# A written-out instruction order replanned: VectorE's SBUF steps given a later planned start beside GpSimd, and one weight load held back

## The chip, the cores and the metric

The kernel runs on one core of a Trainium2 chip. The time is device microseconds from start to end of one execution; for each kernel the median of several runs is given. Lower is better. The engines are named as in the profile: PE is TensorE (matmul), DVE is VectorE, ACT is ScalarE, POOL is GpSimd, SP is SyncE, which issues most DMAs here.

## The reference

The reference is one transformer-like block on 4096 positions of 640 channels, in float32. A first network mixes positions in the frequency domain; a second one is a gated feed-forward network. Both sit behind a layer norm that is scaled and shifted by a condition vector `c`, and both are added back through a gate. Cut to what matters:

```python
mod = (silu(c) @ w_mod).reshape(1, 6, 1, 640)        # sa, ca, ga, sb, cb, gb
h = layernorm(x) * (1 + ca) + sa
z = rfft2(h)                                          # 4096 positions, 4 blocks of 160 channels
h1 = relu(z @ w1 + b1); o = softshrink(h1 @ w2 + b2)  # complex, block by block
x = x + ga * irfft2(o)
h = layernorm(x) * (1 + cb) + sb
x = x + gb * ((silu(h @ w_gate) * (h @ w_up)) @ w_down)   # 640 -> 1728 -> 640
```

## The kernel before, in words

TensorE multiplies in a reduced float32 format. To keep full accuracy, every operand is split in two: ScalarE writes the rounded high part (`high`), VectorE subtracts it from the original and writes the low part (`low`), and each product is made of three matmuls (high x high, high x low, low x high). A product therefore needs one VectorE operation with two inputs in SBUF for each of its operands. The many L1481 (`wb`, gate and up weights), L1671 and L1680 (down weights), L1748 (`chl`, frequency rows), L1870 (`ho`, left sides), L2125, L2274 and L2157 (activations) lines of the profile are such differences.

The first network fills the first 300 us or so of the profile. The change does not touch it. The second network goes through five tiles of rows (`TL`: two of 512 rows, three of 1024). In each tile it goes through 14 units of gate and up weights (`WG`; unit 4 is the up weight of the second pair of column blocks) and seven pieces of down weights. The seventh piece is the narrow rest: rows 1536 to 1727 of `w_down`. From the third tile on a variant with seven products in place of eight is used for most blocks; it needs sums and differences of blocks, which GpSimd makes.

At the same time the rows of the next tile are prepared. For each row, the frequency-domain result is read back (`cr`), multiplied by the gate on GpSimd (L1741, `gated`), split, transformed on TensorE (L1758), added to `x` on VectorE (L1762), normed, transposed, split again (L1870), written to DRAM (`hs`) and read back as the left side `h` of the next tile (L1951).

All of this stands in one instruction order which the Python program writes out by hand with a planner. It keeps a clock `now` (TensorE's planned time), the planned time at which each engine is free (`free["A"]`, `["V"]`, `["P"]` for GpSimd, `["S"]` for SyncE), and the planned end of each step (`done`). Side work is put into `Chain`s of `Step(engine, duration, function, deps, key, ...)`. After each stretch of matmuls `slot` moves the clock and `sweep` goes through the chains in a fixed order: `tries` emits a chain's first step if what it depends on is planned to be done by about now and if its engine could start it no later than `AHEAD` (0.9 us for VectorE and SyncE, 1.2 us for GpSimd) from now. A step that TensorE needs at once is emitted by `until` and `force`. TensorE's own side work (engine `"T"`: L1758 and the transposes) is emitted only some time after its inputs are planned to be ready. Operations that read TensorE's results are emitted directly and planned by `core`. Nothing of the planner runs on the chip: it only decides in which order each engine's queue is filled. On the chip each engine works through its queue in that order and waits at semaphores for its data.

`prep_wd(t, p)` makes the steps for piece `p` of the down weights in tile `t`. For the narrow rest in the first tile (`own`) these are: a load in three DMAs (L1655, L1657), two folds on GpSimd that multiply the gate vector into the weights (L1662), four conversions on ScalarE (L1682), four differences on VectorE (L1680) and a store of the folded weights for later tiles (L1685). The chain `first_w` that holds them is the last in the order of the chains. Before the change its load depends on nothing, so it is planned first of all. The key `("wb", 0, 4, 1)` is the second half of the split of unit 4 in the first tile.

Of the kernel before, what the change touches and what calls it, by code (L numbers as in the profile page):

```python
# [13 lines left out]
P = 128  # L14
D = 640
S = 4096
# [158 lines left out]
def body(tc, x, w1, b1, w2, b2, wg, wu, wd, c, wm, k_fa, k_tb, k_tx, k_bx, k_ga, k_ge, k_id, out, dbg=None):  # L175
    nc = tc.nc
    pe, act, dve, pool = nc.tensor, nc.scalar, nc.vector, nc.gpsimd
# [27 lines left out]
    with ExitStack() as top:  # L205
# [34 lines left out]
        with ExitStack() as af:  # L240
# [351 lines left out]
            wdf = {}  # L592
# [552 lines left out]
        with ExitStack() as ff:  # L1145
# [37 lines left out]
            now = [0.0]  # L1183
            free = dict.fromkeys("AVPSDG", 0.0)
# [11 lines left out]
            bufs |= {f"p{q}": 2 for q in range(4)}  # L1196
            room = {k: [0.0] * n for k, n in bufs.items()}

            class Step:
                def __init__(self, e, n, f, deps=(), key=None, use=(), free=(), bulk=0.0):  # L1200
                    self.e, self.n, self.f, self.deps, self.key = e, n, f, deps, key
                    self.use, self.free, self.bulk = use, free, bulk

            class Chain:
# [25 lines left out]
                def run(self):  # L1230
                    t = self.at()
                    st = self.steps.pop(0)
                    for tag in st.use:
                        room[tag].remove(min(room[tag]))
                    e = st.e
                    if e == "T":
                        wait_pe(t)
                        st.f()
                        now[0] += st.n
                        end = now[0] + 0.17 + LAT  # L1240
                    elif e == "N":
                        end = t
                    elif e in "SG":
                        q = "S" if e == "S" else "P"
                        issue = max(free[q], now[0], t) + (0.45 if e == "S" else 0.6)
                        st.f()
                        free[q] = issue
                        free["D"] = max(free["D"], issue + 0.9) + st.n
                        end = free["D"] + 0.9
                    else:  # L1250
                        start = max(free[e], now[0], t)
                        st.f()
                        free[e] = start + st.n
                        end = free[e] + LAT
                    if st.key is not None:
                        done[st.key] = end
                    for tag in st.free:
                        room[tag].append(end)

            def wait_pe(t):  # L1260
                if t > now[0]:
                    now[0] = t + min(2.0, t - now[0])

            def tries(c):
                while c.steps:
                    st = c.steps[0]
                    e = st.e
                    t = c.at()
                    if t is None or t > now[0] + (EARLY[e] if e != "T" else -0.8 if ("tile", NS) in done else
                                                  -1.8 if st.deps[0][0] == "xn" else -0.8):  # L1270
                        return
                    if e == "T" and not (room["p1"] or room["p2"] or room["p3"]):
                        return
                    if e not in "TN":
                        start = max(free["P" if e == "G" else e], now[0], t)
                        if start > now[0] + AHEAD[e]:
                            return
                        if e == "A" and start + st.n > quiet[0] + 0.45:
                            return
                        if st.bulk and free["D"] > now[0] + st.bulk:  # L1280
                            return
                    c.run()
# [9 lines left out]
            def sweep():  # L1292
                held = False
                for c in tails + chains:
                    if c in rows:

                        if held:
                            continue
                        tries(c)
                        held = len(c.steps) > 0  # L1300
                    else:
                        tries(c)
                tails[:] = [c for c in tails if c.steps]
# [249 lines left out]
            wds = {}  # L1553
# [77 lines left out]
            def prep_wd(t, p):  # L1631
                if (t, min(p, NPR - 1)) in D7:
                    return block_loads(t, p)
                made = t or p < 4

                own = t == 0 and p == NPR
# [48 lines left out]
                    nc.sync.dma_start(wdd[p], wdraw[t, p].rearrange("p a b -> p (a b)"))  # L1685

                raw_ = ("wdr", t, p)
                out = [Step("S", 1.7, load, (("wds", p),) if made else (), raw_, ("h4", "h7", "e") if own else ("wd",))]
                for f in range(0 if made else 2):
                    out += [Step("P", 2.2, lambda f=f: fold(f), (raw_, ("gbb", 0), ("gbb", 1)), ("wdg", p, f))]  # L1690
                ready = (raw_,) if made else (("wdg", p, 0), ("wdg", p, 1))
# [5 lines left out]
                for f in range(0 if p == NPR else 2):  # L1697
# [3 lines left out]
                                 free=("wd",) if f and made else ())]  # L1701
# [916 lines left out]
            for t in range(NT):  # L2618
                for p in range(NPR + 1):
                    (first_w if (t, p) == (0, NPR) else down_w).add(prep_wd(t, p))  # L2620
                if t >= NS:
                    for n in range(NW):
                        if WG[n][0] != "s":
                            wtl.add([load_t(t, n, i) for i in range(2)])
                if t:
                    left_l.add(load_h(t))
                    x2_l.add(load_x2(t))
                    row_chain(t)
# [55 lines left out]
```

## Time and profile before

| what | value |
|---|---|
| median of 3 runs before | 1421.38 us (1418.54 to 1427.64) |
| the profiled execution, its own time | 1417.8 us |
| its span, first to last instruction | 1415.7 us |
| TensorE busy | 1380.6 us |
| VectorE busy | 1075.7 us |
| ScalarE busy | 698.0 us |
| GpSimd busy | 517.5 us |
| HBM read and written | 233.37 MB and 104.86 MB |

A line of a timeline gives the start and the length in us, the engine, the line of the kernel, the operation, output <- inputs, shape and count, and in brackets how long the engine had stood idle and for whom. Lines of several like instructions are merged (`x2`); their length then runs from the first start to the last end. A line of the view of waits gives the total, the number and the longest of the waits. A line of the table of windows gives the busy time of each engine in the window, the granted TensorE clock, the busy share of the DMA engines and GB/s. In the list of DMA issues the last column is the median time from issue to landing.

### The profile page before, as it was taken

What the parts mean: (1) busy time and instruction counts of PE and PEld (TensorE: products, weight loads), DVE (VectorE), ACT (ScalarE), POOL (GpSimd) and SP (SyncE); (2) the same over time, 40 slices, a digit from 0 to 9 for tenths busy, and PEclk for the clock granted to TensorE, in tenths of its full rate; (3) what the DMA queues carried; (4) which work ended last, traced back from release to release, by engine and by line L of the source; (5) the groups of instructions that cost most, each with busy time, mean ns of one, the idle gap of its engine ahead of it and who ended that gap; (6) DMA issues with size and microseconds to landing.
All of it is one profiled execution on the core that took longest, in us unless ns stands there. A gap on an engine that the chain in (4) does not pass through costs nothing.

```text
span 1415.7 us, 22483 instructions
## 1 busy us (share of the span) xinstructions
PE 1380.6 (98%) x8096; PEld 1205.4 (85%) x8096; DVE 1075.7 (76%) x1882; ACT 698.0 (49%) x1350; POOL 517.5 (37%) x592
## 2 busy tenths in 40 slices
PE   6999999989999999998999999999999999999998
PEld 2699999968888888887889888888888898888888
DVE  8888898798888799758787786476677756666666
ACT  6855555555454565544554455354443415443431
POOL 5300330135474355222444344232434403555431
PEclk9999999999999999999999999999999999999999
DMA  9976677557769978996766779974664795444441
GB/s 373 321 246 207 213 245 241 190 166 263 258 225 333 340 260 301 364 363 217 238 206 238 236 243 359 351 245 159 211 200 142 251 362 202 149 144 153 162 143 75
DMA packets 135519, 339.71 MB, mean 240 GB/s; under 512 B 19152, under 2 KB 56080, under 8 KB 129648
## 3 DMA queue, kind: packets, MB, share of 16 engines
q1 hardware_dynamic: 127264, 322.15, 65.7%
q0 software_dynamic: 6272, 12.85, 2.8%
q10 hardware_dynamic: 1872, 3.28, 0.6%
q8 instruction: 64, 1.05, 0.3%
q14 instruction: 47, 0.39, 0.1%
HBM read 233.37 MB, written 104.86 MB: 239 GB/s over the span
## 4 chain that ended last, share of the span: by engine, by line
PE 82%; DVE 10%; DMA 4%; issue 2%; ACT 1%; POOL 0%; SPq 0%; DVEq 0%; ACTq 0%; POOLq 0%
PE pd L2543 13%; PE pw L2224 8%; PE pw L2226 8%; PE pw L2225 8%; PE pc L803 5%; PE pd_X L2406 5%; PE pl L735 5%; PE pg L2090 3%; PE pg L2089 3%; PE pg L2088 3%; PE pd_Y L2406 2%; PE pw L2237 2%; PE pw L2235 2%; PE pw L2236 2%; PE pb L639 2%
## 5 line engine op out<-in xcount | busy, mean ns | idle before, releaser
L2543 PE MATMUL pd<-wdh,a 128*128 128x320 f32 x896 | 205.7, 310 | 0.5 <-DVE x L2512 0.5
L1481 DVE TENSOR_TENSOR wb<-r,wb 128x512 fp32r<-128x512 f32 (+3 forms) x133 | 147.1, 1111 | 11.9 <-ACT wb L1478 11.7
L2543 PEld LDWEIGHTS pd<-wdh,a 128*128 128x128 f32 x896 | 151.8, 188 | 1.6 <-DVE x L2512 0.8
L2543 PE MATMUL pd<-wdl,a 128*128 128x320 f32 x448 | 138.4, 309 | 0.0
L2512 DVE TENSOR_TENSOR x<-x,pd 128x320 f32<-128x320 f32 x224 | 101.9, 478 | 34.9 <-PE pd L2543 30.2
L2224 PE MATMUL pw<-h,wt 128*128 128x512 f32 x312 | 124.3, 399 | 3.4 <-ACT s_x L2243 2.2
L2226 PE MATMUL pw<-h,wt 128*128 128x512 f32 x312 | 122.4, 392 | 0.0
L2225 PE MATMUL pw<-h,wt 128*128 128x512 f32 x312 | 122.1, 391 | 0.0
L1478 ACT ACTIVATE wb<-r 128x512 fp32r<-128x512 f32 (+3 forms) x141 | 97.2, 705 | 33.0 <-PE pw L2237 22.8
L2090 PE MATMUL pg<-ht,wb 128*128 128x512 f32 x260 | 101.5, 390 | 3.2 <-DVE wb L1481 3.2
L2088 PE MATMUL pg<-ht,wb 128*128 128x512 f32 x260 | 102.7, 395 | 0.0
L2089 PE MATMUL pg<-ht,wb 128*128 128x512 f32 x260 | 101.5, 390 | 0.0
L2226 PE MATMUL pw<-h,wb 128*128 128x512 f32 x234 | 91.3, 390 | 1.5 <-DVE wb L1481 1.5
L2224 PE MATMUL pw<-h,wb 128*128 128x512 f32 x234 | 91.4, 391 | 0.0
L2225 PE MATMUL pw<-h,wb 128*128 128x512 f32 x234 | 91.3, 390 | 0.0
L2381 DVE TENSOR_TENSOR x<-x,pd_X 128x320 f32<-128x320 f32 x160 | 72.7, 485 | 16.3 <-PE pd_X L2406 15.9
L2543 PEld LDWEIGHTS pd<-wdl,a 128*128 128x128 f32 x448 | 84.1, 188 | 0.6
L2224 PEld LDWEIGHTS pw<-h,wt 128*128 128x128 f32 x312 | 58.6, 188 | 16.5 <-ACT s_x L2243 2.6
L2226 PEld LDWEIGHTS pw<-h,wt 128*128 128x128 f32 x312 | 58.6, 188 | 13.4
L2225 PEld LDWEIGHTS pw<-h,wt 128*128 128x128 f32 x312 | 58.9, 189 | 11.9
L2250 DVE TENSOR_TENSOR s_x<-pw,s_x 128x512 f32<-128x512 f32 x39 | 26.7, 685 | 55.5 <-PE pw L2237 55.5
L1741 POOL TENSOR_TENSOR cr<-cr,gab 128x640 f32<-128x640 f32 x28 | 47.3, 1692 | 57.2 <-DMA cr<-s 48.6
(353 smaller groups left out, 3778.4 us busy)
## 6 DMA issues: line engine op xcount, KB each, us to landing
wt<-td SPq DMA_DIRECT2D x78, 512.0 KB, 4.9
hs<-ho SPq DMA_DIRECT2D x52, 512.0 KB, 4.9
h<-hs SPq DMA_DIRECT2D x24, 1024.0 KB, 9.0
r<-in_B_w_up_dram SPq DMA_DIRECT2D x30, 640.0 KB, 4.4
r<-in_B_w_gate_dram SPq DMA_DIRECT2D x29, 640.0 KB, 4.7
wdr<-wdd SPq DMA_DIRECT2D x20, 640.0 KB, 5.8
td<-wt SPq DMA_DIRECT2D x25, 512.0 KB, 6.0
g<-s SPq DMA_DIRECT2D x7, 1280.0 KB, 7.1
```

Source lines behind the costliest of these rows:

```text
L1478: act.activation(wbs[t, n][:, 0, ks, e], raw_of(ks, e), AF.Copy)
L1481: (pool if onp else dve).tensor_tensor(wbs[t, n][:, 1, ks, e], raw_of(ks, e), f32(wbs[t, n][:, 0, ks, e]), op=OP.subtract)
L2088: mm(b, wh, hh, start=(kk == 0), stop=False)
L2089: mm(b, wh, hl, start=False, stop=False)
L2090: mm(b, wl, hh, start=False, stop=(kk == 4))
L2224: mm(b, w(0, kp), a[:, kp, 0], start=start and kp == 0, stop=False, skip_group_check=not start)
L2225: mm(b, w(0, kp), a[:, kp, 1], start=False, stop=False, skip_group_check=not start)
L2226: mm(b, w(1, kp), a[:, kp, 0], start=False, stop=kp == 1, skip_group_check=not start)
L2381: dve.tensor_tensor(x2, x2, q[:, :320], op=OP.add)
L2406: mm(bk[b, i][:, :320], x, y, start=new and j == 0, stop=j == len(seq) - 1, skip_group_check=not new)
L2512: dve.tensor_tensor(x2[:, e], x2[:, e], x[0][:, :320], op=OP.add)
L2543: mm(pd[g, hf][0][:, :320], l, m, start=i == 0, stop=i == len(s) - 1 and not (last and len(gs) > 1))
```

## The change

In the planner, VectorE steps with the keys `wb`, `tsl`, `wdf`, `chl`, `hl`, `act` and `left` (`shares`) get a later planned start: if GpSimd is planned to be busy beyond the step's own start, 0.4 of that excess is added. `tries` and `run` both use the new start through `begin`. `begin` also has a branch for GpSimd steps, which returns the unchanged start: `0 * port[0] + 1.0 * x` is `x`. In `prep_wd` the load of the narrow rest in the first tile now depends on the second half of the split of unit 4.

```diff
+            port = [0.0]
+
+            def shares(st):
+                return st.e == "V" and st.key is not None and st.key[0] in ("wb", "tsl", "wdf", "chl", "hl", "act", "left")
+
+            def begin(st, t):
+                x = max(free["P" if st.e == "G" else st.e], now[0], t)
+                if shares(st):
+                    return x + 0.4 * max(0.0, free["P"] - x)
+                if st.e == "P" and port[0] - 1.0 < x:
+                    return max(x, 0 * port[0] + 1.0 * x)
+                return x
...
-                        start = max(free[e], now[0], t)
+                        start = begin(st, t)
                         st.f()
                         free[e] = start + st.n
+                        if shares(st):
+                            port[0] = free[e]
...
-                        start = max(free["P" if e == "G" else e], now[0], t)
+                        start = begin(st, t)
                         if start > now[0] + AHEAD[e]:
                             return
...
-                out = [Step("S", 1.7, load, (("wds", p),) if made else (), raw_, ("h4", "h7", "e") if own else ("wd",))]
+                out = [Step("S", 1.7, load, (("wds", p),) if made else (("wb", 0, 4, 1),) if own else (), raw_,
+                            ("h4", "h7", "e") if own else ("wd",))]
```

## The prediction

> **What bounds the kernel now.** I read the page first: the busy shares, then the chain of work that ended last.
>
> ```profile
> span 1415.7 us, 22483 instructions
> PE 1380.6 (98%) x8096; PEld 1205.4 (85%) x8096; DVE 1075.7 (76%) x1882; ACT 698.0 (49%) x1350; POOL 517.5 (37%) x592
> ...
> PE 82%; DVE 10%; DMA 4%; issue 2%; ACT 1%; POOL 0%; SPq 0%; DVEq 0%; ACTq 0%; POOLq 0%
> ```
>
> TensorE is busy for 98% of the span and carries 82% of the chain. The change alters neither the matmuls nor their number, so it can move the time only through TensorE's waits. The planner orders only the second network; its stage, from about 304 us to the last matmuls, stands in one row of the table of windows:
>
> ```profile
> core 0: us, PE busy (x) PEld busy (x) DVE busy (x) ACT busy (x) POOL busy (x), PEclk, DMA share, GB/s
> 304.00:1404.00 1100.00, 1086.56 (x5744) 957.39 (x5743) 813.85 (x1334) 511.88 (x940) 446.46 (x460) 1.00 0.69 238
> ```
>
> TensorE stands still for 1100.00 - 1086.56 = 13.4 us there, at a granted clock of 1.00. That is the ceiling of any gain, 0.95% of the time. Next I asked where these microseconds are. The timelines of TensorE, VectorE (DVE) and GpSimd (POOL) at the stage's start show the largest one:
>
> ```profile
> 307.27 0.39 PE L2088 MATMUL pg<-ht,wb 128*128 128x512 f32 x1
> 307.50 0.39 PE L2089 MATMUL pg<-ht,wb 128*128 128x512 f32 x1
> 311.07 0.50 PE L2090 MATMUL pg<-ht,wb 128*128 128x512 f32 x1 [3.19 <-DVE wb L1481]
> ```
> ```profile
> 305.52 5.83 DVE L1481 TENSOR_TENSOR wb<-r,wb 128x768 fp32r<-128x768 f32 x2
> ```
> ```profile
> 304.99 0.61 POOL L1733 DMA_DIRECT2D gt<-in_k_ga_dram  x1
> 305.62 1.58 POOL L1662 TENSOR_TENSOR w<-w,gbb 128x640 f32<-128x640 f32 x1
> 307.16 1.55 POOL L1741 TENSOR_TENSOR cr<-cr,gab 128x640 f32<-128x640 f32 x1
> 308.66 1.53 POOL L1662 TENSOR_TENSOR w<-w,gbb 128x640 f32<-128x640 f32 x1
> ```
>
> The matmul at 311.07 waits for the second part of a weight split (L1481). VectorE starts that split at 305.52; it is released only at 311.07. GpSimd runs without a gap from 304.99 to 308.66 + 1.53 = 310.19, and the split ends about 0.9 us later, as if it could begin its work only then. The two L1662 lines are the folds of the narrow rest, which the change holds. The other waits of TensorE, from 330 us on, in the view of waits:
>
> ```profile
> PE pw L2224 <- ACT s_x L2243: 2.2, 1, 2.2
> PE py L1758 <- DVE chl L1748: 2.2, 3, 0.9
> PE pw L2226 <- DVE wb L1481: 1.5, 1, 1.5
> PE py L1758 <- issue: 0.8, 1, 0.8
> PE pw L2235 <- ACT s_z L2243: 0.7, 1, 0.7
> PE pw L2224 <- ACT s_y L2243: 0.7, 1, 0.7
> PE pd L2543 <- DVE x L2512: 0.5, 1, 0.5
> PE pd_X L2406 <- DVE s_z L2250: 0.5, 1, 0.5
> PE pw L2224 <- DMA wt<-td: 0.4, 1, 0.4
> ```
>
> They sum to 9.5 us. The 1.5 us has the same form as the first stall:
>
> ```profile
> 645.90 0.50 PE L2226 MATMUL pw<-h,wb 128*128 128x512 f32 x1 [1.55 <-DVE wb L1481]
> 639.92 5.92 DVE L1481 TENSOR_TENSOR wb<-r,wb 128x768 fp32r<-128x768 f32 x1
> 639.40 0.59 POOL L1733 DMA_DIRECT2D gt<-in_k_ga_dram  x1
> 640.01 0.75 POOL L1850 TENSOR_TENSOR sa<-h,sa 128x256 f32<-128x256 f32 x1
> 640.71 1.29 POOL L2271 TENSOR_TENSOR sg<-s_v,sg 128x512 f32<-128x512 f32 x1
> 641.96 3.07 POOL L1741 TENSOR_TENSOR cr<-cr,gab 128x640 f32<-128x640 f32 x2
> ```
>
> Again one split lasts 5.92 us, to 0.8 us past the end of a closed run of GpSimd work (645.03). The 2.2 us wait for s_x follows soon after, behind work queued after this split. So VectorE's operations with both inputs in SBUF, started beside GpSimd, account for the 3.2 us and for 2.2 (chl) + 1.5 + 2.2 = 5.9 of the 9.5.
>
> **Part 1: the hold.** The load of the narrow rest is planned only after the split of unit 4. Three loads leave the head of SyncE's queue, two folds leave GpSimd's, and four conversions (ScalarE), four differences (VectorE, L1680) and one store (SyncE) follow them. Of the GpSimd run at the start only L1741 is left: it may take the first fold's place at 305.62 and end at 307.17. The split then ends 0.88 us after that, as 311.07 stands after 310.19, so TensorE goes on at 308.05. Its pace is 307.50 - 307.27 = 0.23 us a matmul, so it wants to go on at 307.73. A stall of 0.3 us remains of 311.07 - 307.73 = 3.3: a gain of **3.0 us**; the ends are 3.3 (L1741 lands elsewhere) and 0 (the planner fills the gap with other GpSimd work). The next load for the same buffer starts when this split ends, so it comes as much earlier as TensorE does, and the gain is not given back at the next unit.
>
> [...]
>
> What the folds meet at their new place:
>
> ```profile
> 326.79 0.33 SPq L1456 DMA_DIRECT2D r<-in_B_w_up_dram  x1
> wdr<-wdd SPq DMA_DIRECT2D x2, 640.0 KB, 6.3
> 332.21 0.96 DVE L1481 TENSOR_TENSOR wb<-r,wb 128x768 fp32r<-128x768 f32 x1 [1.25 <-ACT wb L1478]
> 335.21 0.39 PE L2088 MATMUL pg<-ht,wb 128*128 128x512 f32 x1
> 331.41 0.74 POOL L1525 TENSOR_TENSOR ts<-r 128x256 f32<-128x256 f32 x1 [0.93 <-DMA r<-in_B_w_up_dram]
> 332.23 1.53 POOL L1525 TENSOR_TENSOR ts<-r,ts 128x256 f32<-128x256 f32 x1
> 333.73 0.73 POOL L1525 TENSOR_TENSOR ts<-r 128x256 f32<-128x256 f32 x1
> ```
>
> The split of unit 4 ends just before the load at 326.79, which takes over its buffer; that load stands ahead of the narrow rest's in the order of chains. With some 6.3 us to landing, as loads of this size need here, the folds run at about 333 to 336 (330 to 333 when all is 3 us earlier). SyncE's queue behind the three loads holds a store of rows and one of weight sums, neither of which TensorE wants soon. On VectorE the split at 332.21 could be caught: it ends at 333.17, and its part is wanted after six matmuls of unit 5, 335.21 + 6 x 0.23 = 336.6. That leaves 3.4 us of cover against 1.58 + 1.53 = 3.1 us of folds. Alone they cost nothing; behind the three L1525 (0.74 + 1.53 + 0.73 = 3.0) they would cost up to 3.1 + 3.0 - 3.4 = 2.7. I take **0.5 us**, near the covered end, because the planner still sees these neighbours. The wait is one of the plan: it adds no semaphore, only an issue order. The result is wanted at the end of the first tile.
>
> **Part 2: VectorE's steps planned later.** A step with key wb, tsl, wdf, chl, hl, act or left is planned to start later by 0.4 of the time that GpSimd is planned ahead. Nothing is added on the chip. The new guard for GpSimd's own steps returns the start it was given, so it is inert. Two things follow. TensorE's optional work (the row transforms L1758) is planned further behind its chl difference, which speaks to the 2.2 us of the second wait. And a step whose planned start is over 0.9 us ahead is held back, so fewer long SBUF operations stand in front of VectorE's reads of PSUM. No row prices this. The ends are the whole 5.9 us gained and, by the two starved splits above, as much lost at one or two new places. I take 0.4 of the 5.9 as removed, since 0.4 of the overlap is planned for: 2.4 us, and set half of it, 1.2, against it for new collisions of a reshuffled order. Net gain **1.2 us**.
>
> [...]
>
> **Sum.** -3.0 + 0.5 - 1.2 = -3.7 us. The profiled execution took 1417.8 us (its span is 1415.7) and would take 1414.1. The median of the runs before is 1421.4, 3.6 above the profiled execution, so the forecast is 1421.4 - 3.7 = **1417.7 us**.
>
> **The rivals.**
>
> *Gain given back.* The folds meet the split at the new place (2.7), or a new closed GpSimd run catches a split elsewhere (a second 1.5 to 3.2). Net 0: 1421. For it: two such accidents exist in 13.4 us of waits, and nothing in the change forbids them. Against it: the cover of 3.4 us.
>
> *Slower: the second network's third tile starts late.* Its left sides go through DRAM, and the row steps that make them contain differences which are now planned later:
>
> ```profile
> q1 hardware_dynamic: 3665, 13.59, 97.9%
> h<-hs SPq DMA_DIRECT2D x6, 1024.0 KB, 10.2
> 596.84 1.30 SPq L1951 DMA_DIRECT2D h<-hs  x2
> 615.88 0.40 PE L2224 MATMUL pw<-h,wt 128*128 128x512 f32 x1
> ```
>
> From 575 to 612 us the main queue moves data 97.9% of the time, so lateness cannot be made up. The last two loads are out by 596.84 + 1.30 = 598.1 and land by about 598.1 + 10.2 = 608.3; the product that reads the first of them starts at 615.88. The point from which this decides is 7.6 us of slip. A held split loses at most 0.4 of a closed GpSimd run, 0.4 x (645.03 - 640.01) = 2.0 us; with two in series in each of the tile's four pairs of rows, 16.0. Then TensorE waits 8.4, and with -3.7 or, without part 2, -2.5 the net is +4.7 to +5.9: 1426.5. Against it: the planner still forces what TensorE needs next. Beyond 1% it would take a slip of some 25 us.
>
> *The plan hardly moves.* Where VectorE is planned as far ahead as GpSimd the delay is zero; then only the hold acts: -2.5, 1418.9.
>
> *All VectorE-made waits go.* -3.0 + 0.5 - 5.9 = -8.4: 1413.0.
>
> **Chances.** Forecast 0.45; given back 0.22; slower at the third tile or by an accident like it 0.13; plan unmoved 0.08; all waits go 0.12. The range reaches from 1410 (the last case, less the 2.8 us by which the lowest run before, 1418.5, lies below the median) to 1428 (the slow case and 1.5 us for the same spread). A run of this kernel can tell about 1% (14 us) from no change. Faster by over 1% would need more than all of TensorE's idle time in the stage: 0.02. Slower by over 1%: the far end of the slow case, 0.05. Within 1%: 0.93.
>
> **What would show it.** Right: no wait of 3 us near 308, the split there ending within 1 us of a single GpSimd step, L1662 on w near 330; fewer waits of L1758 for chl; TensorE's idle time after 304 near 10 us. Wrong: a new split of over 3 us with a TensorE wait behind it, above all near 330; TensorE waiting for h after 608; the two rows of 1.5 and 2.2 us still there, which would leave part 2 at nothing.

## The result, and the profile after

The changed kernel takes 1413.11 us (median of 13 runs, 1409.94 to 1415.6), the kernel before 1422.41 us in the same comparison (13 runs, 1417.95 to 1427.64). The ratio is 0.9932 with a 95% interval of 0.9922 to 0.9943: 9.3 us less, 0.68%. The forecast was 1417.7 us, within 1%.

The page of the changed kernel, its row in the table of windows and TensorE's waits in the second network:

```profile
span 1410.2 us, 22459 instructions
...
PE 1381.1 (98%) x8096; PEld 1207.8 (86%) x8096; DVE 1075.4 (76%) x1882; ACT 698.9 (50%) x1350; POOL 518.9 (37%) x592
```
```profile
304.00:1400.00 1096.00, 1088.52 (x5758) 961.37 (x5757) 815.26 (x1339) 513.15 (x941) 447.92 (x460) 1.00 0.69 240
```
```profile
PE pd L2559 <- ACT sg L2126: 2.2, 1, 2.2
PE pw L2240 <- ACT s_y L2259: 1.2, 1, 1.2
PE pw L2251 <- ACT s_z L2259: 1.1, 1, 1.1
PE pw L2240 <- DMA wt<-td: 1.0, 1, 1.0
PE py L1774 <- DVE chl L1764: 1.0, 2, 0.5
PE pw L2240 <- DVE x L2528: 0.5, 1, 0.5
PE pg L2106 <- DVE wb L1496: 0.2, 1, 0.2
```

The line numbers have moved by up to 16 (L1481 is now L1496, L1758 is L1774, L1662 is L1677). The waits now sum to 7.2 us, against 3.2 + 9.5 = 12.7. In the row of windows TensorE stands still for 1096.00 - 1088.52 = 7.5 us, against 13.4 before and the 10 that the prediction gave as its sign. The pair of 1.5 (wb) and 2.2 us (s_x) is gone, and the row transforms wait 1.0 us for chl in place of 2.2. The start of the second network, on TensorE, VectorE and GpSimd:

```profile
308.68 0.50 PE L2106 MATMUL pg<-ht,wb 128*128 128x512 f32 x1 [0.21 <-DVE wb L1496]
```
```profile
305.38 3.25 DVE L1496 TENSOR_TENSOR wb<-r,wb 128x512 fp32r<-128x512 f32 x2 [0.55 <-ACT wb L1493]
```
```profile
305.59 0.61 POOL L1749 DMA_DIRECT2D gt<-in_k_ga_dram  x1
306.22 1.58 POOL L1757 TENSOR_TENSOR cr<-cr,gab 128x640 f32<-128x640 f32 x1
307.74 0.58 POOL L1749 DMA_DIRECT2D gt<-in_k_ga_dram  x1
...
329.38 3.50 POOL L1677 TENSOR_TENSOR w<-w,gbb 128x640 f32<-128x640 f32 x2
```

One GpSimd step is left at the start. The two splits end at 305.38 + 3.25 = 308.63, 0.83 us after that step (306.22 + 1.58 = 307.80), and TensorE's wait has fallen from 3.19 to 0.21 us. The folds run at 329.38. A new wait stands just beside them. TensorE's row, two of ScalarE's, and the granted clock (the last but two column) after the wait:

```profile
330.76 0.41 PE L2559 MATMUL pd<-wdh,a 128*128 128x320 f32 x1 [2.18 <-ACT sg L2126]
```
```profile
328.78 0.92 ACT L1805 ACTIVATE xn<-x,nm_b,rs_b 128x640 f32<-128x640 f32 x1 [3.38 <-POOL nm_b L1796]
330.13 0.57 ACT L2126 ACTIVATE sg<-pg 128x512 f32<-128x512 f32 x1
```
```profile
331.00:335.00 4.00, 4.00 (x18) 4.00 (x18) 3.97 (x10) 1.58 (x4) 3.76 (x6) 0.57 0.96 383
332.00:334.00 2.00, 2.00 (x9) 2.00 (x9) 1.97 (x7) 0.32 (x1) 1.83 (x4) 0.50 1.00 413
```

The new order puts a row's norm (`xn`) into ScalarE's queue ahead of the read that frees TensorE's PSUM bank; the norm waits for GpSimd, and TensorE waits with it. Behind the wait the clock is at 0.50 from 332 to 334. From 331 to 335 it averages 0.57, so it was at 0.5 for 4 x 0.43 / 0.5 = 3.4 us, which cost 1.7. TensorE counts as busy in these microseconds (4.00 of 4.00), so no view of waits shows them.

### The profile page after: what moved, and what is told of

The parts are those of the page before. It is cut to its first block, busy times and chain, and to the rows that moved or that the text cites. A ratio compares the mean times of both kernels' runs of the same rounds, so it can differ in the third digit from the quotient of the medians.

```text
span 1410.2 us, 22459 instructions
## 1 busy us (share of the span) xinstructions
PE 1381.1 (98%) x8096; PEld 1207.8 (86%) x8096; DVE 1075.4 (76%) x1882; ACT 698.9 (50%) x1350; POOL 518.9 (37%) x592
## 4 chain that ended last, share of the span: by engine, by line
PE 86%; DVE 5%; DMA 3%; ACT 2%; issue 2%; POOL 1%; SPq 0%; DVEq 0%; ACTq 0%; POOLq 0%
PE pd L2559 14%; PE pw L2240 8%; PE pw L2242 8%; PE pw L2241 8%; PE pd_X L2422 5%; PE pc L803 5%; PE pl L735 4%; PE pg L2105 4%; PE pg L2104 4%; PE pg L2106 4%; PE pd_Y L2422 3%; PE pw L2253 2%; PE pw L2251 2%; PE pw L2252 2%; PE pb L639 2%
## 5 line engine op out<-in xcount | busy, mean ns | idle before, releaser
L1496 DVE TENSOR_TENSOR wb<-r,wb 128x512 fp32r<-128x512 f32 (+3 forms) x133 | 140.5, 1064 | 10.2 <-ACT wb L1493 10.0
L858 POOL DMA_DIRECT2D s<-co x28 | 15.5, 555 | 140.7 <-ACT co L852 140.1
L2259 ACT ACTIVATE s_x<-pw 128x512 f32<-128x512 f32 x39 | 23.2, 595 | 85.7 <-PE pw L2242 83.8
```

The lines of the kernel that those rows point to most:

```text
L1496: (pool if onp else dve).tensor_tensor(wbs[t, n][:, 1, ks, e], raw_of(ks, e), f32(wbs[t, n][:, 0, ks, e]), op=OP.subtract)
```

## The experiments

Two theories stood against each other from the start. In the first, the start's wait is the folds' doing and the planned delay removes VectorE's waits by its own mechanism. In the second, the delay only makes another order, and each order is a draw. The expectations name them by letters: A is the first; B says that the hold alone makes the gain; C and later E are the second; D says that the delay has a steady effect that grows with its share. All medians and ratios are against the kernel before in the same comparison.

| kernel | median us | ratio to before | 95% interval | span of its profile |
|---|---|---|---|---|
| the full change | 1413.11 | 0.9932 | 0.9922 to 0.9943 | 1410.2 |
| hold alone | 1425.47 | 1.0006 | 0.9994 to 1.0019 | 1423.6 |
| delay alone | 1421.34 | 0.9979 | 0.9965 to 0.9993 | 1420.1 |
| hold, delay for chl only | 1418.4 | 0.9968 | 0.9952 to 0.9984 | 1416.5 |
| hold, delay for all but chl | 1422.09 | 0.9988 | 0.9972 to 1.0005 | 1421.4 |
| full, share 0.2 | 1431.49 | 1.0058 | 1.0038 to 1.0078 | 1434.0 |
| full, share 1.0 | 1456.57 | 1.0231 | 1.0205 to 1.0256 | 1453.3 |
| hold alone, latency 0.13 | 1414.65 | 0.9934 | 0.9913 to 0.9954 | 1413.3 |
| hold alone, latency 0.11 | 1425.42 | 1.0011 | 0.9995 to 1.0028 | 1422.4 |
| full, latency 0.13 | 1417.59 | 0.9962 | 0.9945 to 0.9979 | 1413.3 |
| full, latency 0.11 | 1415.08 | 0.9945 | 0.992 to 0.997 | 1413.0 |
| folds held, load not | 1426.13 | 1.0013 | 0.9994 to 1.0031 | 1423.4 |
| before, once more | 1424.63 (one run) | | | 1422.5 |

**The two parts apart.** Hold alone is the kernel before with the last hunk of the diff; delay alone is the changed kernel without it.

```diff
 # hold alone: before, with
-                out = [Step("S", 1.7, load, (("wds", p),) if made else (), raw_, ...
+                out = [Step("S", 1.7, load, (("wds", p),) if made else (("wb", 0, 4, 1),) if own else (), raw_, ...
```

> Only the load of the narrow rest is held back; VectorE's steps are planned as before. Theory A (the start's stall is the folds' doing, and the planned delay brings the rest): 2.5 to 3.5 us below the kernel before, the wait of 3.2 us near 308 down to about 0.3, and the waits behind long splits later on (645, 652 before) still there in some form. Theory B (the hold alone made nearly all of the gain): 7 to 9 us below. Theory C (any new order loses the accidents of the old one): waits from 330 us on also shrink, 5 to 8 us below.

> Only the planned delay of VectorE's SBUF steps; the narrow rest is loaded first as before. Theory A: 5 to 7 us below the kernel before, with the 3.2 us wait near 308 still there since both folds run in the same closed GpSimd run. Theory B: within 2 us of the kernel before. Theory C: 2 to 6 us below, with waits at other places.

Neither brings the gain: the hold alone is level with before, where every theory had expected at least 2.5 us, and the delay alone is 0.2% faster. TensorE's waits of the hold alone:

```profile
PE py L1759 <- DVE chl L1749: 4.2, 4, 2.0
PE pd L2544 <- DVE a L2126: 2.7, 2, 2.5
PE pw L2225 <- ACT s_x L2244: 2.2, 1, 2.2
PE pt L1823 <- ACT xn L1790: 1.6, 1, 1.6
PE pw L2227 <- DVE wb L1481: 1.5, 1, 1.5
PE pt L1823 <- ACT sg L2111: 1.1, 1, 1.1
...
PE pg L2091 <- DVE wb L1481: 0.2, 1, 0.2
```

The wait at the start is gone here too (0.2), and none has come near 330. But the row transforms wait 4.2 us where they waited 2.2, and 2.7 + 1.6 + 1.1 us stand at places that had no wait before. Moving one load has changed the whole order behind it, and the new order waits more. The pair of 1.5 and 2.2 us is still there. The delay alone keeps the 3.2 us at the start, as theory A had it.

**Parts of the delay.** The list of keys in `shares` is cut to chl, or chl is taken out.

```diff
-                return st.e == "V" and st.key is not None and st.key[0] in ("wb", "tsl", "wdf", "chl", "hl", "act", "left")
+                return st.e == "V" and st.key is not None and st.key[0] in ("chl",)
```

> The hold, and the planned delay for the chl differences alone (28 steps). Theory A (part of the gain is that the row transforms L1758 are planned further behind their chl difference): TensorE's waits of L1758 for chl fall from 2.2 to under 1 us, the long splits remain, 4 to 5 us below the kernel before. If the delay of the other differences carries the gain: as the hold alone.

> The hold, and the planned delay for all of the listed keys but chl. Theory A: most of the gain of the full change, 6 to 8 us below the kernel before, with L1758's waits for chl back at about 2 us. If only the chl delay matters: as the hold alone, about 3 us below.

The delay for chl alone gives half of the gain, 0.32%, which is about what theory A expected, but not where it should: L1774 still waits 4.7 us for chl, more than before, so the number was met by accident. The rest of the keys give about nothing (the interval includes 1), where theory A expected 6 to 8 us. The parts don't add up to the whole.

**The size of the share.** 0.4 becomes 0.2 and 1.0.

> The full change with 0.2 in place of 0.4 as the share of GpSimd's planned excess. Theory D (the planned delay has an effect in its own right, in the direction of less waiting, that grows with the share): 3 to 6 us below the kernel before, between the hold alone (0) and the full change (9). Theory E (each planned order is a draw; the share only reshuffles): anywhere from 2 us above to 9 us below, with no order in the share.

> The full change with 1.0 in place of 0.4. Theory D: as low as the full change or lower, 8 to 12 us below the kernel before, since in the traces a split starved by a closed GpSimd run waits for all of it. Theory E: anywhere from 2 us above to 9 us below.

0.2 is 0.6% slower than before, 1.0 is 2.3% slower; 0.4 lies between them and is faster than both. No effect that grows with the share looks like this. Both lie above the range of theory E too, which ended at 2 us above. With 0.2 no single place explains the loss: TensorE's waits sum to 21.6 us, the longest of them 4.0. The loss at 1.0 has a mechanism of its own. TensorE's row, the first loads (`tl`) that it waits for, and the stores of block B22, the last of which goes out just ahead of those loads; below, the same stores in the changed kernel (the numbers of a store are its shortest, median and longest length in ns, then the first and the last start in us):

```profile
1167.74 0.64 PE L2422 MATMUL pd_Y<-tl,a 128*128 128x320 f32 x1 [22.35 <-DMA tl<-wsd]
```
```profile
1162.65 2.46 SPq L1589 DMA_DIRECT2D tl<-wsd  x2
L1629 SPq DMA_DIRECT2D wsd<-B22hl x7: 513/519/887, 550.6 to 1162.0; - x7
```
```profile
L1629 SPq DMA_DIRECT2D wsd<-B22hl x7: 512/519/519, 516.6 to 1035.6; - x7
```

The sums of the down weights' blocks are a side chain of low priority, with a VectorE split in each step. The last block is stored at 1162 in place of 1036. The loads that need all blocks follow it at 1162.65, and TensorE waits 22 us. That the larger delay holds each of these splits back until its start is near, while other steps go first, is read from the planner; no run shows it by itself.

**Orders without any delay.** The planner's latency between steps (`LAT`), which has nothing to do with GpSimd, is moved by 0.01 us.

```diff
-            LAT = 0.12
+            LAT = 0.13
```

> The hold alone, with a planner's constant that has nothing to do with GpSimd changed a little: the latency between steps 0.13 in place of 0.12 us. It shows how much a mere reshuffle moves the time. Theory D: within 2 us of the hold alone (which stood level with the kernel before). Theory E: several us away from it, 2 us above to 8 us below the kernel before. In both the wait near 308 stays at about 0.3 us.

> The full change with the same small change of the latency constant. Theory D: stays 7 to 11 us below the kernel before. Theory E: gives back a part, 1 to 7 us below.

> The hold alone, latency constant 0.11 in place of 0.12: one more order without any planned delay. If each order is a draw (theory E, which the runs before this one favour): between 8 us above and 10 us below the kernel before, not bound to the hold alone (level) nor to the hold with 0.13 (9.6 below). If the hold alone has a value of its own that the first run of it missed: 3 to 10 us below. The wait near 308 stays at about 0.3 us.

> The full change, latency constant 0.11. Theory E: between 8 us above and 10 us below the kernel before. If the share of 0.4 makes orders with less waiting whatever the other constants: 6 to 10 us below, as with 0.12 and 0.13.

With 0.13 the hold alone is 0.66% faster than before, as fast as the full change within the intervals, and no VectorE step is planned later in it. That is 9.6 us, more than the 8 that theory E allowed: its range was too narrow on this side as well. With 0.11 it is level again. The full change gains 0.38% to 0.68% with the three constants. So an order as good as that of the full change is to be had without the delay, and 10 us lie between neighbours of the same rule. That three of three orders with 0.4 are faster, and one of three without, leaves room for an effect of the delay; six orders don't settle it, and the orders at 0.2 and 1.0 speak against a steady one.

What the orders with a gain have in common stands near 640 us. Splits with their GpSimd neighbours, first in the hold alone (latency 0.12; the second of two splits), then in the changed kernel (both):

```profile
647.58 5.93 DVE L1481 TENSOR_TENSOR wb<-r,wb 128x768 fp32r<-128x768 f32 x1
```
```profile
647.06 0.59 POOL L1734 DMA_DIRECT2D gt<-in_k_ga_dram  x1
647.67 0.75 POOL L1851 TENSOR_TENSOR sa<-h,sa 128x256 f32<-128x256 f32 x1
648.37 1.29 POOL L2272 TENSOR_TENSOR sg<-s_v,sg 128x512 f32<-128x512 f32 x1
649.62 3.07 POOL L1742 TENSOR_TENSOR cr<-cr,gab 128x640 f32<-128x640 f32 x2
```
```profile
633.96 3.43 DVE L1496 TENSOR_TENSOR wb<-r,wb 128x512 fp32r<-128x512 f32 x2
```
```profile
633.59 1.29 POOL L2287 TENSOR_TENSOR sg<-s_z,sg 128x512 f32<-128x512 f32 x1 [1.29 <-ACT wb L1493]
634.84 1.74 POOL L2287 TENSOR_TENSOR sg<-s_v,sg 128x512 f32<-128x512 f32 x1
```

The one split takes 5.93 us beside the closed GpSimd run; in the changed kernel two splits together take 3.43 beside two steps. The waits of 1.5 (wb) and 2.2 us (s_x) behind the first of these stand in the kernel before, in the hold alone and in the kernel with the folds held, and as 1.0 and 2.6 in the hold with latency 0.11; none of the four kernels with the largest gains (the full change with each latency, the hold with 0.13) has such a pair. This is what they share, not shown to be the whole of the difference: the delay for all keys but chl has no wait for s_x either and is level with before.

**Folds or loads.** The kernel before, with the load first as there, and only the two folds held back.

```diff
-                    out += [Step("P", 2.2, lambda f=f: fold(f), (raw_, ("gbb", 0), ("gbb", 1)), ("wdg", p, f))]
+                    out += [Step("P", 2.2, lambda f=f: fold(f), (raw_, ("gbb", 0), ("gbb", 1)) + ((("wb", 0, 4, 1),) if own else ()),
+                                 ("wdg", p, f))]
```

> The kernel before with the narrow rest loaded first as there, but its two folds on GpSimd, not its load, held until the split of unit 4 is planned. If the folds are what starves the split near 308: TensorE's wait there falls from 3.2 to about 0.3 us, as with the load held. If the three loads at the head of SyncE's queue were the cause: it stays at 3.2. The total is a draw like the others.

```profile
308.65 0.50 PE L2091 MATMUL pg<-ht,wb 128*128 128x512 f32 x1 [0.19 <-DVE wb L1481]
```

The wait is 0.19 us. It was the folds on GpSimd, not the three loads at the head of SyncE's queue, that held the split up. The total is level with before, as for the hold alone.

**Before, once more.**

> The kernel before, unchanged, profiled once more. The same waits at the same places in TensorE's order, within 0.3 us each. If its spread from run to run comes from the granted clock falling to half after some of the longer waits, in some executions and not in others: one or more stretches at 0.5 behind the waits near 308, 645 or 652, and a span longer than 1415.7 us by 1 to 3 us for each; none of them stood in the first profile. If not: no such stretch, and the span within 2 us of the first.

Its longest waits, TensorE's matmuls behind the wait at the start and at the wait for wt, and the granted clock behind three of the waits:

```profile
PE pg L2090 <- DVE wb L1481: 3.2, 1, 3.2
PE py L1758 <- DVE chl L1748: 2.3, 2, 1.4
PE pw L2224 <- ACT s_x L2243: 2.2, 1, 2.2
PE pw L2224 <- DMA wt<-td: 2.0, 1, 2.0
PE pw L2226 <- DVE wb L1481: 1.5, 1, 1.5
```
```profile
311.02 0.79 PE L2090 MATMUL pg<-ht,wb 128*128 128x512 f32 x1 [3.21 <-DVE wb L1481]
311.61 0.63 PE L2088 MATMUL pg<-ht,wb 128*128 128x512 f32 x1
312.04 0.63 PE L2089 MATMUL pg<-ht,wb 128*128 128x512 f32 x1
627.50 0.66 PE L2224 MATMUL pw<-h,wt 128*128 128x512 f32 x1 [1.97 <-DMA wt<-td]
```
```profile
307.00:311.00 4.00, 0.82 (x4) 0.35 (x2) 4.00 (x2) 3.65 (x8) 3.14 (x3) 0.90 0.00 0
311.00:318.00 7.00, 6.98 (x18) 5.53 (x19) 5.88 (x11) 0.99 (x3) 0.07 (x1) 0.57 0.82 243
627.00:632.00 5.00, 4.50 (x15) 3.67 (x16) 0.00 (x0) 0.76 (x2) 0.00 (x0) 0.66 0.47 179
658.00:662.00 4.00, 4.00 (x12) 3.11 (x11) 1.96 (x4) 2.88 (x6) 0.00 (x0) 0.57 0.64 218
```

The waits are the old ones (the one for wt is 1.6 us longer, not within the 0.3 expected), yet the span is 1422.5 in place of 1415.7. After the wait of 3.2 us the matmuls come 0.43 us apart (311.61, 312.04) where the pace is 0.23; the clock is 0.57 on average over 7 us, so at 0.5 for 7 x 0.43 / 0.5 = 6.0 us, which cost 3.0. A second such stretch follows the wait of 1.97 us for wt (0.66 over 5 us: 5 x 0.34 / 0.5 = 3.4 us, 1.7 lost), a third the wait of 2.2 us for s_x (0.57 over 4 us: 3.4 us, 1.7 lost). The first profile, on which the prediction rests, had the clock at 1.00 throughout the stage. The three stretches cost 6.4 us, and all waits together are 1.0 us longer (13.7 against 12.7). That makes 7.4, a little more than the 6.8 us between the two profiles.

## Why the prediction was right, and where it was not

The total lay in the range, but its two parts did not come as they were added up. The hold alone is level with before (1.0006), where -2.5 us was forecast; the delay on top of it brings 0.9932 against 1.0006, some 10.5 us, where 1.2 was taken. That the two together came near is luck.

- **The start's wait (part 1).** Right to 0.1 us: a remaining stall of 0.3 was forecast and 0.21 measured. The split that was to end 0.88 us after the one GpSimd step left ended 0.83 us after it. Holding the folds alone does the same (0.19). So the folds set the split's length, though in the kernel before the split started first (305.52, the first fold at 305.62).
- **Its price.** Mis-sized: 3.0 us was counted, the idle time. In the second profile of before, the half clock behind the wait cost 3.0 more. Nor was the 3.6 us between the first profile and the median a constant of the measurement, as the sum took it: the second profile shows it to be made, in large part, of half-clock stretches that the first happened not to have.
- **The distance from -3.7 to -9.3.** No single cause makes most of these 5.6 us. About 2.2 are half clock: the mean granted clock is 0.9969 in the 66 executions of before that were measured beside the experiments and 0.9985 in the 13 of the changed kernel, and if all that is missing is time at work at half clock, it cost 4.4 and 2.2 us. Another 1.8 are waiting: between the first two profiles TensorE's waits fell by 12.7 - 7.2 = 5.5 us, where the sum had 3.7. The remaining 1.6 are open. The executions with a mean clock of 1.000 agree that the clock is not the whole of it: their median span is 1416.6 us in seven of before and 1408.8 in three of the changed kernel, 7.8 less.
- **The folds' new place.** 0.5 us was taken; in the hold alone no wait of over 0.4 us stands there, the cover of 3.4 us held. The 2.18 us near 330 of the changed kernel belongs to the queue of ScalarE, which the prediction didn't look at; it stands in four of the delayed orders (the changed kernel, all keys but chl, the share of 0.2, latency 0.11).
- **The planned delay (part 2).** The direction came out, the reason didn't. "0.4 of the overlap planned for removes 0.4 of the waits" fails: 0.2 made the kernel slower, 1.0 much slower, and an order without any delay gains as much. The term was one order's luck or little more; a net 1.2 us with ends of nearly 6 on both sides was too narrow, as the 0.2 kernel shows.
- **The rivals.** "Gain given back" is what the hold alone does, with waits at other places than the one named. The slow rival's kind, splits held back until something that passes through DRAM comes late, is what the share of 1.0 shows, at the blocks of down weights and not at the third tile's left sides. "The plan hardly moves" is out: the order changes on every engine. The guard for GpSimd's steps is inert as forecast, by its code: it returns `x` in either case.

## What to carry to other kernels

In a kernel whose order comes from a greedy planner, a change of a planning rule is measured as one draw of an order. Draw its neighbours (a constant moved by a hundredth) with the rule and without it before the rule is credited. Waits of TensorE of 1.97, 2.18 and 3.21 us had a second price in the clock here (1.7, 1.7 and 3.0 us), which the view of waits doesn't show: read the granted clock behind a wait, in more than one profile. And where VectorE's two-input SBUF work feeds TensorE, look for one that starts while GpSimd is issuing a DMA with several of its steps queued behind; those at 305.52 and 639.92 of the kernel before took 5.50 and 5.92 us. Holding the folds back shortened the first to 2.51 us; moving the DMA issue was not tried.

## What the runs showed of the hardware

VectorE operations with two SBUF inputs outlasted one GpSimd step and more: the split at 639.92 of the kernel before took 5.92 us and ended 0.8 us behind the last of four steps, and in the changed kernel the second of the two splits at 305.38 ended 0.83 us behind a single one. Not every closed run did this. Another place of the kernel before:

```profile
345.31 1.81 POOL L1741 TENSOR_TENSOR cr<-cr,gab 128x640 f32<-128x640 f32 x1 [5.60 <-DMA cr<-s]
347.08 1.44 POOL L1525 TENSOR_TENSOR ts<-r,ts 128x256 f32<-128x256 f32 x1
345.73 2.21 DVE L1481 TENSOR_TENSOR wb<-r,wb 128x768 fp32r<-128x768 f32 x1
```

This split ended at 347.94, 0.82 us behind the first step, and the second step, begun at 347.08, took 1.44 us where the shortest of its kind in this trace took 0.73, as if the split had got its turn between the two. What differs is what GpSimd was doing when the split started. Here it ran a tensor operation; at 305.52 and 639.92 it was issuing a DMA (304.99 to 305.60, 639.40 to 639.99). Counted from 304 us on in the traces of the kernel before and the changed one, where a GpSimd tensor operation followed within 0.1 us: of 272 VectorE operations with two SBUF inputs that started during a GpSimd tensor operation, 262 ended before the following one did; of 20 that started during a GpSimd DMA issue, 17 ended after it. Why a DMA issue goes with this difference is not shown.

The granted clock fell to half in or behind waits of 1.97, 2.2 and 3.21 us (second profile of before) and 2.18 us (changed kernel), and didn't behind the waits of 3.19 and 2.22 us in the first profile of before. In the delay alone it was 0.50 from 312.5 to 318.5, behind the wait of 3.2 us at the start. So waits of about 2.2 and 3.2 us were followed by half clock in one execution and not in another; what decides it is not shown. Worked out from the windows, the stretches at 0.5 are 3.4 us long in the changed kernel and 0.8 + 6.0 = 6.8 (behind 3.21 us), 3.4 and 3.4 in the second profile of before.
